# A long convolution and an MLP in one kernel: k and v loaded in rows of four tokens, and the short convolution split at the phase wrap

## The chip, the cores and the metric

The kernel runs on one core of a Trainium2 chip. The core has a tensor engine for matrix products (PE, with weight loads listed apart as PEld), a vector engine (DVE), a scalar engine (ACT), GpSimd (POOL) and a queue engine (SP), which here only issues DMA transfers. On-chip memory is SBUF (128 partitions); matrix products are written to PSUM[...]. The metric is device time in microseconds, and the figure compared is the median of several runs. One further execution is recorded by the hardware profiler, and the profile and the trace come from it.

## The reference

There are two blocks, one after the other, over 2048 tokens of 512 channels, all in bfloat16. Block A normalises the input to get q, and then computes

```
k_shift[s] = sum over t of k_pad[s + t] * shift_k[:, 3 - t]     (4 taps, causal, per channel)
kv         = k_shift * v
y          = irfft( rfft(kv padded to 4096) * rfft(ssm_k padded to 4096) )[:2048]
h          = x + q * (y + kv * ssm_D)
```

Block B is `h2 = h + relu(layernorm(h) @ w1) @ w2` with 1376 hidden columns. The part that the change touches is the first two lines: the four-tap convolution of k along the tokens, with one weight per channel and tap, and the product with v.

## The kernel before

The transforms of length 4096 are written as matrix products. Both operands of the convolution, `ssm_k` and `kv`, go through the same steps: a transpose on PE (`to_rows`, line 281), a first transform stage (`stage1`, line 310) and a second one (`stage2`, lines 328 and 330). Then the spectra are multiplied (lines 452 and 462), the inverse transform runs (lines 609, 675 and 687), the result is gated with q (lines 658 and 660), and the two layers of the MLP follow (lines 714 and 744).

The kernel is written under a manual schedule: each engine executes its instructions in the order in which the program emits them, and waits only for the data and buffers that each instruction names.

**The loads.** SP issues, in this order: the whole `ssm_k` (`sk`, 2 MB, line 96), then alternately a transposing load of 512 tokens of k and of v, four of each (lines 115, 117 and 118), and then two small loads of `ssm_D` (`draw`, line 121). The tap weights `wsh` (4 KB) are issued on ACT's queue (line 98). A transposing load puts channels on the partitions: `kT[c]` and `vT[c]` have 128 channels on the partitions, four channel groups, and the tokens of the chunk along the free axis. Each k chunk after the first is loaded with the 16 tokens ahead of it, so that the taps can reach back over the border of the chunk; in the first chunk these 16 columns are zeros (line 112).

**The tap weights.** POOL multiplies the identity by the weights and so makes `wdiag`, a diagonal 128 x 128 matrix for each of four channel groups and four taps (line 238). The products are made for two channel groups, then the table `f1` is split into a high and a low part (lines 241 to 243), and then the other two groups follow. After that POOL copies the split tables to `f2` (line 247) and negates tables for the second stage (line 250).

**The tap products.** `taps(c, h)` handles chunk c and the two channel groups 2h and 2h + 1. For each group PE adds up four products of a diagonal matrix with 512 columns of `kT[c]`, each tap reading one column further back (line 369). DVE multiplies the bank by `vT[c]` and writes the result into `kvp2`, a view of the buffer `sk`, in the order that the transform wants (line 372). The two banks are `pk0` and `pk1`; the next call of `taps` needs them free.

**The order around the change.** PE runs 22 matmuls to warm up, then transposes `sk` (32 instructions), and then goes through eight rounds. Round gb calls `taps(gb // 2, gb % 2)` and then `stage1` on a part of the `ssm_k` data. After the eighth round PE transposes the finished `kv` into `xfl`, and the second stages begin. DVE works on the tables of angles at the start (lines 198, 189, 44, 46 and 222), evacuates the first transposes (line 284), makes the second half of a table (lines 222 and 189), and only then starts the tap products of line 372. ACT makes the sine tables (line 193) and evacuates most of `stage1`.

Of the kernel before, what the change touches and what calls it, by code (L numbers as in the profile page):

```python
# [9 lines left out]
ALU = mybir.AluOpType  # L10
BF16 = mybir.dt.bfloat16
F32 = mybir.dt.float32
# [3 lines left out]
P = 128  # L16
# [40 lines left out]
def kernel(  # L57
# [13 lines left out]
    nc = tc.nc  # L71
    _, S, D = A_q.shape
    DFF = B_w1.shape[1]
    KS = A_shift_k.shape[1]
    assert S == 2048 and D == 512 and KS == 4, "kernel is specialised to S=2048, D=512, ks=4"
    NT = 16
    DC = D // P
    NFC = (DFF + P - 1) // P
    x_d, k_d, v_d, out_d = A_q[0], A_k[0], A_v[0], out[0]
# [5 lines left out]
    consts = pl.push("consts")  # L85
    slotA = pl.push("slotA")
    vp = pl.push("vp")
    early = pl.push("early")
    wp = pl.push("wp", side="right")
    kvp = pl.push("kvp", side="right")  # L90
# [2 lines left out]


    sk = early.tile([P, DC, S], BF16, name="sk")
    nc.sync.dma_start(out=sk[:], in_=A_ssm_k.rearrange("(c p) t -> p c t", p=P))
    wsh = consts.tile([P, DC, KS], BF16, name="wsh")
    nc.scalar.dma_start(out=wsh[:], in_=A_shift_k.rearrange("(r p) j -> p r j", p=P))
    dtab = consts.tile([P, 64, DC], BF16, name="dtab")
    draw = consts.tile([P, DC, 64], BF16, name="draw")  # L100
    vT = [vp.tile([P, DC, 512], BF16, name=f"vT{c}") for c in range(4)]
    CH = 512
    kT = [(kvp if c < 2 else early).tile([P, DC, CH + 16], BF16, name=f"kT{c}") for c in range(4)]
    wdiag = kvp.tile([P, DC, KS, P], BF16, name="wdiag")

    idle = vT[3][:, 0, :]
    nc.vector.memset(idle, 0.0)
    warm = psum_t.tile([P, 512], F32, tag="pk0", name="warm")
    for _ in range(22):
        nc.tensor.matmul(out=warm[:], lhsT=idle[:, 0:P], rhs=idle, start=True, stop=True)  # L110

    nc.vector.memset(kT[0][:, :, 0:16], 0.0)
    for c in range(4):
        if c == 0:
            nc.sync.dma_start_transpose(out=kT[c][:, :, 16:CH + 16], in_=k_d[0:CH, :])  # L115
        else:
            nc.sync.dma_start_transpose(out=kT[c][:], in_=k_d[CH * c - 16:CH * c + CH, :])  # L117
        nc.sync.dma_start_transpose(out=vT[c][:], in_=v_d[CH * c:CH * c + CH, :])  # L118
    for dp in range(2):
        src = bass.AP(tensor=A_ssm_D.tensor, offset=A_ssm_D.offset + 64 * dp, ap=[[0, 64], [P, DC], [1, 64]])  # L120
        nc.sync.dma_start(out=draw[64 * dp:64 * dp + 64, :, :], in_=src)
# [84 lines left out]
    t1 = early.tile([P, 64], I32, name="f1_t")  # L206
# [30 lines left out]
    for rg in range(DC):  # L237
        nc.gpsimd.tensor_tensor(out=wdiag[:, rg, :, :], in0=ident[:].unsqueeze(1).to_broadcast([P, KS, P]),
                                in1=wsh[:, rg, :].unsqueeze(2).to_broadcast([P, KS, P]), op=ALU.mult)
# [34 lines left out]
    def tap_bank(i, shape, dtype, name):  # L274
        return psum_t.tile(shape, dtype, tag=f"pk{i}", name=name)
# [55 lines left out]
                             skip_group_check=True)  # L331


    kfl = early.tile([P, 64, 2, 64], BF16, name="kfl")
    sk32 = sk[:].rearrange("p c t -> p (c t)").bitcast(F32).rearrange("p (x m) -> p x m", m=32)
    kv32 = sk[:].rearrange("p c t -> p (c t)").bitcast(F32).rearrange("p (m x) -> p m x", m=32)

# [25 lines left out]

    kvp2 = sk[:].rearrange("p c t -> p (c t)").rearrange("p (m c a e) -> p m c a e", m=32, c=DC, e=2)
    def taps(c, h):
        pss = [tap_bank(i, [P, 512], F32, "pkv") for i in range(2)]
        for i in range(2):
            for j in range(KS):
                nc.tensor.matmul(out=pss[i][:], lhsT=wdiag[:, 2 * h + i, j, :],  # L369
                                 rhs=kT[c][:, 2 * h + i, 16 - j:CH + 16 - j], start=(j == 0), stop=(j == KS - 1))  # L370
        for i in range(2):
            nc.vector.tensor_tensor(out=kvp2[:, :, 2 * h + i, 8 * c:8 * c + 8, :].rearrange("p m a e -> p a m e"),
                                    in0=pss[i][:].rearrange("p (a m e) -> p a m e", a=8, e=2),
                                    in1=vT[c][:, 2 * h + i, :].rearrange("p (a m e) -> p a m e", a=8, e=2),
                                    op=ALU.mult)

    for gb in range(8):
        taps(gb // 2, gb % 2)
        stage1(kfl, a1k_of, gb, ("AA", "AD")[gb % 2], pairs=(gb == 2))
        if gb < 6:  # L380
            cc_part()
        if gb == 1:
            negated(22, 32)
# [458 lines left out]
```

## Time and profile before

| what | value |
|---|---|
| median of 8 runs | 204.6 us (204.02 to 208.47) |
| the profiled execution's own time | 204.62 us |
| its span in the profile | 202.5 us |
| PE busy | 191.4 us (95%), 2209 matmuls |
| DVE busy | 144.9 us (72%) |
| ACT busy | 128.8 us (64%) |
| POOL busy | 85.5 us (42%) |
| tap products on PE (line 369) | 64 instructions, 15.2 us busy, mean 380 ns |
| tap products on DVE (line 372) | 16 instructions, 10.7 us busy, mean 688 ns |
| transposing loads of k and v on SP | 8 instructions, first at 1.26 us, last at 26.07 us |

The span is the time from the first to the last instruction in the trace; the profiled execution's own time contains some 2.1 us around it. Busy time is summed per engine. Matmuls overlap one another in the array, so 380 ns is the length of one from start to end and not the distance to the next. A number after a releaser ("<-") is the time for which the engine stood idle just before the instruction, and the name is what ended the wait according to the profile; when an instruction waits for several things, the profile names the last of them that it sees.

### The profile page before, as it was taken

The page shows a single profiled execution, that of the slowest core. Times are in us where ns is not written, and L with a number is a line of the kernel's source. Part 1 is how long each engine was busy: PE and PEld are TensorE (multiplying, and loading weights), DVE is VectorE, ACT ScalarE, POOL GpSimd, SP SyncE. Part 2 cuts the span into 40 slices and gives each one's busy share as a digit, 9 for nine tenths or more (in the row PEclk, how much of TensorE's full clock was granted, in tenths as well). Part 3 has the DMA queues.
Part 4 walks back from the last instruction along what each step waited for, and adds up shares of the span by engine and source line. Part 5 has one row for each costly group of instructions (what it writes and reads, how often), then busy time and mean ns, then how long its engine had stood idle before and what let it go on. Part 6 is the DMA issues. An engine that isn't in the chain of part 4 may idle for free.

```text
span 202.5 us, 5318 instructions
## 1 busy us (share of the span) xinstructions
PE 191.4 (95%) x2209; PEld 136.0 (67%) x2209; DVE 144.9 (72%) x238; ACT 128.8 (64%) x199; POOL 85.5 (42%) x121
## 2 busy tenths in 40 slices
PE   7797989999988999999999999999999999999991
PEld 2474545999987989988998877545664556544451
DVE  7988776887877998898994698959477117652131
ACT  2668898778785988885979964925570583026300
POOL 7199995000006999994959284200120002002000
PEclk9999999999999999999999999999999999999999
DMA  5999992000000007809980669753481802140011
GB/s 174 342 215 120 203 171 56 3 5 3 3 3 5 0 9 184 288 24 218 259 203 18 108 91 186 141 103 103 91 155 43 107 10 52 32 112 14 0 52 52
DMA packets 48491, 20.05 MB, mean 99 GB/s; under 512 B 43380, under 2 KB 46932, under 8 KB 48468
## 3 DMA queue, kind: packets, MB, share of 16 engines
q1 hardware_dynamic: 47940, 19.71, 47.0%
q8 instruction: 17, 0.28, 0.6%
q10 hardware_dynamic: 528, 0.00, 0.1%
q14 instruction: 6, 0.05, 0.1%
HBM read 7.08 MB, written 2.10 MB: 45 GB/s over the span
## 4 chain that ended last, share of the span: by engine, by line
PE 78%; SPq 11%; DMA 3%; ACT 2%; DVE 2%; issue 1%; ACTq 0%
PE ps1m L714 19%; PE ps2m L744 19%; PE psy L462 7%; PE psi L609 7%; PE ps2k L328 4%; SPq L115 4%; PE ps2k L330 4%; SPq L117 4%; SPq L118 4%; PE u L328 4%; PE u L330 3%; DMA kT<-in_A_k_dram 3%; PE pz L687 3%; PE ps L310 2%; PE pst L281 2%; PE pkv L369 2%
## 5 line engine op out<-in xcount | busy, mean ns | idle before, releaser
L729 ACT ACTIVATE h1T<-ps1m 128x512 bf16<-128x512 f32 (+1 forms) x44 | 25.7, 597 | 35.8 <-PE ps1m L714 35.7
L714 PE MATMUL ps1m<-xT,w 128*128 128x512 bf16 (+2 forms) x192 | 43.7, 365 | 0.4 <-DVE xT L660 0.4
L744 PE MATMUL ps2m<-w,h1T 128*128 128x512 bf16 (+3 forms) x187 | 40.8, 368 | 0.0
L687 PE MATMUL pz<-bd,ax 128*128 128x128 f32 x96 | 35.7, 410 | 0.0
L452 POOL TENSOR_TENSOR t<-usb,kf 128x320 fp32r<-128x320 f32 x32 | 28.2, 918 | 2.2 <-ACT usb L448 1.7
L452 DVE TENSOR_TENSOR t<-u,kf 128x704 fp32r<-128x704 f32 x32 | 26.7, 883 | 3.2 <-ACT usb L448 3.0
L748 DVE SCALAR_TENSOR_TENSOR o<-ps2m,rstd,xh 128x512 bf16<-128x512 f32 (+1 forms) x17 | 12.1, 718 | 22.3 <-PE ps2m L744 11.5
L744 PEld LDWEIGHTS <-h1T 128*128 128x128 bf16 (+1 forms) x187 | 16.2, 98 | 16.0
L553 POOL TENSOR_SCALAR rstd<-mv 128x4 f32<-128x4 f32 x8 | 2.5, 317 | 57.2 <-DVE mv L551 57.2
L259 ACT CAST a<-ps 128x1024 fp32r<-128x1024 f32 (+1 forms) x22 | 22.5, 1058 | 3.8 <-PE ps L310 3.8
L714 PEld LDWEIGHTS <-w 128*128 128x128 bf16 (+1 forms) x192 | 15.9, 100 | 12.1 <-DVE xT L660 0.5
L687 PEld LDWEIGHTS pz<-bd,ax 128*128 128x128 f32 x96 | 18.6, 193 | 7.6
L547 DVE BATCH_NORM_STATS2 st<-xh 128x6 f32<-128x512 bf16 x32 | 19.9, 677 | 0.5 <-DMA xh<-xT 0.5
L658 DVE TENSOR_TENSOR qT<-pz,qT 128x1024 bf16<-128x1024 f32 x8 | 9.8, 1220 | 13.7 <-PE pz L687 10.8
L259 ACT CAST kf<-psy 128x512 fp32r<-128x512 f32 x30 | 17.5, 642 | 1.8 <-PE psy L462 0.2
L537 ACT ACTIVATE bd<-ecw,nbias 32x512 fp32r<-32x512 int32 x24 | 17.3, 719 | 0.6
L369 PE MATMUL pkv<-kT,wdiag 128*128 128x512 bf16 x64 | 15.2, 380 | 1.8 <-POOL f_hi L247 1.1
L462 PE MATMUL psy<-t,ipos 128*128 128x512 f32 x48 | 16.0, 395 | 0.0
L261 DVE CAST a<-ps 128x1024 fp32r<-128x1024 f32 (+1 forms) x12 | 13.6, 1136 | 2.6 <-PE ps L310 2.5
L259 ACT CAST ax<-psi 128x1024 fp32r<-128x1024 f32 x13 | 12.4, 1014 | 3.7 <-PE psi L609 3.5
L609 PE MATMUL psi<-dre,kf 128*128 128x256 f32 x60 | 14.6, 286 | 0.0
L609 PE MATMUL psi<-dim,kf 128*128 128x256 f32 x60 | 14.3, 280 | 0.0
(132 smaller groups left out, 392.5 us busy)
## 6 DMA issues: line engine op xcount, KB each, us to landing
sk<-in_A_ssm_k_dram SPq DMA_DIRECT2D x1, 2048.0 KB
xh<-in_A_q_dram SPq DMA_DIRECT2D x16, 128.0 KB
out_dram<-o SPq DMA_DIRECT2D x15, 128.0 KB
w<-in_B_w_dram SPq DMA_DIRECT2D x1, 1376.0 KB
w<-in_B_w_dram SPq DMA_DIRECT2D x1, 1280.0 KB
xh<-xT SPq DMA_TRANSPOSE x8
out_dram<-o SPq DMA_DIRECT2D x2, 64.0 KB
w<-in_B_w_dram SPq DMA_DIRECT2D x1, 96.0 KB
```

The source lines that it names most:

```text
L259: nc.scalar.copy(out=o, in_=i)
L328: nc.tensor.matmul(out=ps[:, kk, :], lhsT=at_k1(w_re, k1), rhs=a_in(2 * k1), start=True, stop=False, skip_group_check=True)
L369: nc.tensor.matmul(out=pss[i][:], lhsT=wdiag[:, 2 * h + i, j, :], rhs=kT[c][:, 2 * h + i, 16 - j:CH + 16 - j], start=(j == 0), stop=(j == ...
L452: eng.tensor_tensor(out=t[:, :, j, :], in0=in0.unsqueeze(1).to_broadcast([P, 2, n, 2]), in1=kfr[:, :, j, ks], op=ALU.mult)
L462: nc.tensor.matmul(out=psy[:], lhsT=m_[:], rhs=t_.rearrange("p j k -> p (j k)"), start=first, stop=not first)
L537: nc.scalar.activation(out=bd[h][rows, :, :, rg, :], in_=ecw[q % 2][rows, :, 256 * h:256 * h + 256].rearrange("p b (j n) -> p b j n", n=32 ...
L547: nc.vector.bn_stats(out=st[:, i, :], in_=src[:, i, :])
L609: nc.tensor.matmul(out=banks[i // 2][:, i % 2, :], lhsT=kf[:, c, 4 * m:4 * m + 4, :].rearrange("p r k -> p (r k)"), rhs=d[:].rearrange("p ...
L687: nc.tensor.matmul(out=pz[:, il, :, a, :], lhsT=ax[:, 64 * rho + n2, :, :].rearrange("p d g -> p (d g)"), rhs=bd[h][:, rho, 4 * il + a, :, ...
L714: nc.tensor.matmul(out=ps1[fc][:fsz, 128 * ii.start:128 * ii.stop].rearrange("p (i t) -> p i t", t=P), lhsT=w1[:, c, fc * P:fc * P + fsz], ...
L729: nc.scalar.activation(out=h1T[:fsz, fc, :], in_=ps1[fc][:fsz, :], func=ACT.Relu)
L744: nc.tensor.matmul(out=ps2[:, 0:w], lhsT=h1T[:ksz, fc, i * P:(i + 1) * P], rhs=w2[:ksz, fc, ds], start=(fc == 0), stop=(fc == NFC - 1))
```

## The change

Four things are changed, and all of them are in the first 35 us.

1. `k` and `v` are read as matrices with 512 rows of 2048 elements, a row holding four consecutive tokens. A chunk is 128 such rows. The transposing load gives, for each of the four positions t in a row (the phase, the token number modulo 4) and each channel group, a block of 128 channels by 128 rows. `kT` and `vT` become one tile each, `[128, 4 phases, 4 channel groups, rows]`. All 512 rows of k stand behind one another in one tile, with 16 columns of zeros ahead, so that the overlap of 16 tokens for each chunk is no longer loaded.
2. Tap j of phase t reads phase t - j. Where t - j is negative, the token lies in the row before: phase t - j + 4, one column earlier. A tap product therefore has two parts, phases j to 3 and phases 0 to j - 1. Tap 0 has only one part with 512 columns; the others have 384 + 128, 256 + 256 and 128 + 384 columns. A call of `taps` has 14 matmuls instead of 8, each with its own weight load.
3. DVE's product with v reads the bank and `vT` by phase and writes to the same places as before.
4. The load of `wsh` is issued on SP ahead of `sk`, instead of on ACT. The tile `kfl`, which `to_rows` fills, is allocated earlier, and the warm-up matmuls read it instead of `vT[3]`.

```diff
+    kfl = early.tile([P, 64, 2, 64], BF16, name="kfl")
+    wsh = consts.tile([P, DC, KS], BF16, name="wsh")
+    nc.sync.dma_start(out=wsh[:], in_=A_shift_k.rearrange("(r p) j -> p r j", p=P))
     nc.sync.dma_start(out=sk[:], in_=A_ssm_k.rearrange("(c p) t -> p c t", p=P))
-    wsh = consts.tile([P, DC, KS], BF16, name="wsh")
-    nc.scalar.dma_start(out=wsh[:], in_=A_shift_k.rearrange("(r p) j -> p r j", p=P))
...
-    vT = [vp.tile([P, DC, 512], BF16, name=f"vT{c}") for c in range(4)]
-    CH = 512
-    kT = [(kvp if c < 2 else early).tile([P, DC, CH + 16], BF16, name=f"kT{c}") for c in range(4)]
+    CM = 128
+    vT = vp.tile([P, 4, DC, 4 * CM], BF16, name="vT")
+    kT = kvp.tile([P, 4, DC, 4 * CM + 16], BF16, name="kT")
...
-    idle = vT[3][:, 0, :]
+    idle = kfl[:, 0:4].rearrange("p g d n -> p (g d n)")
...
-    nc.vector.memset(kT[0][:, :, 0:16], 0.0)
+    nc.vector.memset(kT[:, :, :, 0:16], 0.0)
     for c in range(4):
-        if c == 0:
-            nc.sync.dma_start_transpose(out=kT[c][:, :, 16:CH + 16], in_=k_d[0:CH, :])
-        else:
-            nc.sync.dma_start_transpose(out=kT[c][:], in_=k_d[CH * c - 16:CH * c + CH, :])
-        nc.sync.dma_start_transpose(out=vT[c][:], in_=v_d[CH * c:CH * c + CH, :])
+        for dst, src, at in ((kT, k_d, 16 + CM * c), (vT, v_d, CM * c)):
+            nc.sync.dma_start_transpose(out=dst[:].rearrange("p t r m -> p (t r) m")[:, :, at:at + CM],
+                                        in_=src.rearrange("(m t) d -> m (t d)", t=4)[CM * c:CM * c + CM, :])
...
-        pss = [tap_bank(i, [P, 512], F32, "pkv") for i in range(2)]
+        pss = [tap_bank(i, [P, 4, CM], F32, "pkv") for i in range(2)]
+        at = 16 + CM * c
         for i in range(2):
+            rg = 2 * h + i
             for j in range(KS):
-                nc.tensor.matmul(out=pss[i][:], lhsT=wdiag[:, 2 * h + i, j, :],
-                                 rhs=kT[c][:, 2 * h + i, 16 - j:CH + 16 - j], start=(j == 0), stop=(j == KS - 1))
+                for t0, t1, f0, m0 in ((j, 4, 0, at), (0, j, 4 - j, at - 1)):
+                    if t0 < t1:
+                        nc.tensor.matmul(out=pss[i][:, t0:t1, :], lhsT=wdiag[:, rg, j, :],
+                                         rhs=kT[:, f0:f0 + t1 - t0, rg, m0:m0 + CM], start=(j == 0),
+                                         stop=(j == KS - 1), skip_group_check=True)
         for i in range(2):
-            nc.vector.tensor_tensor(out=kvp2[:, :, 2 * h + i, 8 * c:8 * c + 8, :].rearrange("p m a e -> p a m e"),
-                                    in0=pss[i][:].rearrange("p (a m e) -> p a m e", a=8, e=2),
-                                    in1=vT[c][:, 2 * h + i, :].rearrange("p (a m e) -> p a m e", a=8, e=2),
-                                    op=ALU.mult)
+            rg = 2 * h + i
+            nc.vector.tensor_tensor(
+                out=kvp2[:, :, rg, 8 * c:8 * c + 8, :].rearrange("p (m tp) a e -> p a m tp e", tp=2),
+                in0=pss[i][:].rearrange("p (tp e) (a m) -> p a m tp e", e=2, a=8),
+                in1=vT[:, :, rg, CM * c:CM * c + CM].rearrange("p (tp e) (a m) -> p a m tp e", e=2, a=8), op=ALU.mult)
```

## The prediction

> **What bounds the kernel now.** I first read the page's chain of work that ended last, because only its links move the end:
>
> ```profile
> PE 78%; SPq 11%; DMA 3%; ACT 2%; DVE 2%; issue 1%; ACTq 0%
> ```
>
> PE carries it nearly everywhere; the 11% of SP's queue and the 3% of DMA are the head. So I next asked for the chain in order of time, cut to 0 to 36 us (start, length, what):
>
> ```profile
> 0.72 0.48 SPq L96
> ...
> 1.26 7.53 SPq L115
> ...
> 15.67 4.75 SPq L117
> ...
> 23.68 6.18 DMA kT<-in_A_k_dram
> ...
> 29.90 1.90 PE pkv L369 x8
> 31.81 0.61 PE ps L310 x64
> 32.42 1.88 PE pkv L369 x8
> ...
> 34.33 0.70 DVE sk L372
> ...
> 35.17 0.84 PE pst L281 x6
> ```
>
> SP issues `sk` and then eight transposes, back to back; the last k chunk lands at 29.86, and from there two tap groups lead to 35.17, where the transposes of the tap products start. After 35 us the chain is PE almost throughout (ACT and DVE links of 0.5 to 1.2 us near 110 to 115), and nothing of the diff lies there. So the change in time is, to a first order, how far 35.17 moves.
>
> Is DMA alone late? The timeline of the same stretch says no:
>
> ```profile
> 13.53 1.41 DVE L222 TENSOR_SCALAR w_tc<-w_ts 128x1024 int32<-128x1024 int32 x1
> 14.97 0.69 DVE L189 TENSOR_SCALAR w_tc<-w_tc 128x1024 int32<-128x1024 int32 x1
> 15.58 1.28 DVE L372 TENSOR_TENSOR sk<-pkv,vT 128x512 bf16<-128x512 f32 x2
> 16.32 1.89 PE L369 MATMUL pkv<-kT,wdiag 128*128 128x512 bf16 x8 [1.09 <-POOL f_hi L247]
> 29.90 1.90 PE L369 MATMUL pkv<-kT,wdiag 128*128 128x512 bf16 x8 [0.63 <-DMA kT<-in_A_k_dram]
> 31.65 1.29 DVE L372 TENSOR_TENSOR sk<-pkv,vT 128x512 bf16<-128x512 f32 x2 [1.05 <-DMA vT<-in_A_v_dram]
> ```
>
> PE lost only 1.09 and 0.63 us between 12.7 and 35. The 1.09 is charged to POOL, but tap group 1 needs the bank that DVE's first product frees at 15.58 + 0.69 = 16.27: that wait is DVE's. PE and DMA therefore run within about a microsecond of each other, and help for one alone meets the other soon.
>
> The loads, from the DMA view of 15 to 24 us (40 slices of 0.225 us):
>
> ```profile
> GB/s 87 224 240 201 94 191 24 3 0 0 41 275 291 355 162 0 0 1 8 9 10 174 275 291 279 290 291 287 291 288 269 188 213 74 35 6 8 10 9 213
> q8 instruction: 2, 0.03, 1.5%
> ```
>
> The transposes run at up to 291 GB/s with holes of 0.9 to 1.4 us. Two instruction fetches fall in this view, and I read two of its three holes as theirs (a reading, not shown here); the view of 24 to 34 us has one more hole, near 28.5, and again two fetches.
>
> **What the Trainium skill says.** "DMA: Bandwidth & Descriptors", section Latency and other measured facts, gives transposes 261 GB/s with a non-contiguous middle dimension and 350 to 400 contiguous. Here the peak is 291. The later transposes of 128 rows by 16 blocks, the new shape but read from SBUF, run at 205 to 218 GB/s back to back (DMA view of 120 to 129 us). Two k/v transposes without a hole between them, issued at 8.83 and 11.03, took 2.15 and 2.61 us to issue for 0.52 MB: about the same pace. The trace does not support 350. "SBUF — State Buffer", section Who interferes with whom: DVE and GpSimd share one port pair, and the second to issue blocks for the whole instruction. The trace agrees: L222 took 1.41 us beside POOL's wdiag and 0.69 us earlier, when POOL was idle.
>
> **The change part by part.** Durations are of the profiled execution (own time 204.62, median 204.6: the sum applies to the median as it is).
>
> *wsh ahead of sk on SP.* Its issue leaves ACT's queue, where it hid, and enters SP's: 0.48 plus a gap, 0.54 us before `sk` (0.72 to 1.26). Behind `sk` stand all eight transposes; PE waits for `sk` at 9.05. wsh is 512 pieces of 8 bytes (q10 held 528 packets, 3.4% of 16 engines over 9 us: 0.3 us per engine). That data cost existed before, beside `sk`. But the two draw loads, 512 pieces of 128 bytes, trickle from 31.3 to 34.0: if pieces go out that slowly and `sk` waits, the delay D reaches 0.54 + 2.7 = 3.2. Below, D could be 0.2 if the two issues overlap. I take D = 0.8: the issue and one more quarter microsecond. The ends go into the range.
>
> *wdiag early.* POOL sat idle from 4.79 to 9.22 for wsh. With wsh landing by about 4, the first two wdiag (2.3 us) run from 4.8, the second pair after f1's split near 9.9 (f_f is done at 9.01), ending near 11.9 instead of 14.40. Then L222 at 13.5 no longer meets them: 1.41 becomes 0.69, minus 0.72 us on DVE ahead of the first products. The price: the first pair now meets DVE's table turns (L189, L198, L222, 4.4 to 9.6), 0.7 to 1.4 us by the same collision. DVE finished these at 9.63 and waited for PE's first transpose until 9.78; with `sk` later by D that cover is 0.95, so 0 to 0.45 is left. I take 0.1.
>
> *Tap matmuls.* Per group of taps, four 512-column products (216 ns apart: 8 in 1.89 us, the last 0.38 long) become one of 512, two of 384, two of 256 and two of 128, each with its own weight load; 48 more pairs in all. Spacing: 256 columns take 118 ns (L714: 25 in 3.10 us, the last 0.27); 384 between, 168. 128 columns with a weight load: "TensorE: Matmul & The Clock Gate", section Back-to-back issue gap, gives 81 ns for such pairs (its 216 ns for 512 columns agrees with the trace). Sum 216 + 2x168 + 2x118 + 2x81 = 950 against 864: +86 ns, x16 = 1.4 us, 0.17 per call of taps. Bounds: 11 ns per extra pair (118 less 256 columns at 216/512) gives 0.5; a full weight load of 98 ns each, with no overlap, gives 4.7.
>
> *Products on DVE.* The reads now step over phases in PSUM and vT. L284 already reads PSUM four elements apart by 128 words, 512 elements, in 0.69 us, as L372 does: nothing. For vT's stride I take nothing; the upper bound is doubling, 16 x 0.69, mostly under PE.
>
> *Memsets, tiles.* The kT memset grows from 32 to 128 words, about 0.1 us on DVE, inside the same 0.95 cover. vT[3]'s dependence on the warm-up matmuls goes; these end at 7.6, far ahead of its issue. The order of DMAs and later instructions is the same.
>
> *Transposes.* Same 4.2 MB, less 48 rows of overlap (0.05 MB, 0.2 us), rows of 4 KB instead of 1 KB. I take the same pace with the same holes: all land D later.
>
> *Sum.* PE path: first products at 15.58 + 0.8 + 0.1 - 0.72 = 15.76, so tap group 1 at 16.50 (+0.18). Group 6 was ready at 29.27; plus 0.18 and five groups at 0.17 gives 30.3. DMA path: 29.90 + 0.8 = 30.7, later, so it decides. Then two tap groups, +0.34: 35.17 becomes 36.3, **+1.1 us: 205.7**.
>
> **Rivals.**
> *Faster (0.20).* The long rows, or a hole that misses the last k chunk, bring that chunk before PE arrives. The hole near 28 cost about 1.4 us, and 96 more PE instructions shift the fetches. PE alone then decides. With D = 0.5 and 0.04 per call: tap group 1 at 16.2, group 6 at 29.35 (29.27 - 0.12 + 5x0.04), the end 5.27 + 0.08 later at 34.7: -0.5, 204.1. It needs kT's last chunk by about 29.3 and 128-column pairs near 64 ns. Against it: the SBUF-fed transposes with 4 KB rows are no quicker.
> *No difference (0.15).* The chunk is early, the pairs cost 0.17 per call and D is 0.3: group 1 at 16.0, group 6 at 29.8, the end at 35.4: +0.2, 204.8.
> *One more hole (0.13).* Another 1.4 us in the loads: +2.5, 207.1. For it: more instructions, hence an earlier fetch.
> *Long rows are slow to transpose (0.07).* Sixteen rows of a block now lie 4 KB apart in HBM. At 0.6 us more per chunk, 8 x 0.6 = 4.8: about 210. Nothing in this trace shows it.
>
> **How the numbers follow.** The main forecast has 0.45, its own range 205.1 to 206.7 (D from 0.2 to 1.8). Slower sums to 0.45 + 0.13 + 0.07 = 0.65, same 0.15, faster 0.20. The range 203.9 to 207.6 leaves out the slow rows and the far end of the faster case. Under 0.2% (0.4 us) is what a measurement here cannot tell from no change.
>
> **What would show it.** D: PE's first L281 at about 9.85 instead of 9.05. wdiag: POOL's first L237 near 4.8. L221's second run 0.69 us. 128-column matmuls 70 to 90 ns apart. kT's last chunk near 30.7, with PE waiting. The xfl transposes start near 36.3. I am wrong if `sk` lands as before, if the chunks come 2.0 us apart or less, or if a tap group stays at 1.9 us.

## The result and the profile after

The changed kernel takes 206.1 us (median of 12 runs, 205.65 to 208.32) where the kernel before takes 204.62 (33 runs). The medians lie 1.5 us apart; the ratio of the runs is 1.0089, with a 95% interval of 1.0067 to 1.0112, so the change makes the kernel slower. The profiled execution took 206.27 us, with a span of 204.2 (before: 202.5). The forecast was 205.7, slower.

The difference is made where the prediction looked for it: the transposes of the tap products into `xfl` start at 36.72 us instead of 35.17, 1.55 later, and the span is 1.7 longer. But the road to that point is another one. On the page of the changed kernel, these are the busy line, the chain by engine, and the two groups of `taps`:

```profile
PE 192.3 (94%) x2257; PEld 139.9 (69%) x2257; DVE 150.5 (74%) x238; ACT 129.4 (63%) x199; POOL 87.2 (43%) x121
...
PE 79%; SPq 7%; DVE 6%; DMA 3%; ACT 2%; issue 1%; ACTq 0%; DVEq 0%
...
L376 DVE TENSOR_TENSOR sk<-pkv,vT 128x512 bf16<-128x512 f32 x16 | 16.4, 1066 | 1.3 <-DMA vT<-in_A_v_dram 0.6
L371 PE MATMUL pkv<-kT,wdiag 128*128 128x128 bf16 (+3 forms) x112 | 15.7, 288 | 1.4 <-DVE sk L376 1.4
```

The same two groups in the kernel before:

```profile
L372 DVE TENSOR_TENSOR sk<-pkv,vT 128x512 bf16<-128x512 f32 x16 | 10.7, 688 | 5.0 <-PE pkv L369 3.5 <-DMA vT<-in_A_v_dram 1.5
L369 PE MATMUL pkv<-kT,wdiag 128*128 128x512 bf16 x64 | 15.2, 380 | 1.8 <-POOL f_hi L247 1.1
```

One number stands out: DVE's product with v takes 1066 ns instead of 688, on the same 512 elements, 16 times: 16.4 us instead of 10.7. DVE's total busy time grew by 5.6 us (144.9 to 150.5), which is this line. The 48 extra matmuls, on the other hand, added 0.5 us of busy PE (15.2 to 15.7). The DVE share of the chain went from 2% to 6%. PE does not stand idle longer before its taps than it did (1.4 us against 1.8), but all of this wait is now for a bank that DVE has not emptied.

The chain of the changed kernel in order of time (start, length, what), from the loads to the `xfl` transposes:

```profile
14.62 6.80 DMA vT<-in_A_v_dram
...
21.51 1.06 DVE sk L376
...
22.61 1.05 PE pkv L371 x7
...
23.69 2.09 DVE sk L376 x2
25.78 0.86 DVE a L260
...
26.82 1.08 DVE sk L376
...
27.95 2.02 PE pkv L371 x14
...
31.04 1.86 PE pkv L371 x14
...
33.51 1.00 PE pkv L371 x7
...
34.53 2.06 DVE sk L376 x2
...
36.72 3.88 PE pst L280 x32
```

In the kernel before, the last chunk of k ended this stretch and PE went straight through two groups of taps. Now a chunk of v comes first: it lands at 21.42, DVE takes it up at 21.51, and from there DVE and PE hand the lead to each other. (DVE waited for this chunk in the kernel before too. The trace keeps the times at which transfers land: there it was 20.64, and DVE's product started at 20.73 after 0.57 us of idle time. The profile charges that wait to PE, whose bank had been complete since 19.80.) PE waits for a bank that DVE has not yet emptied, and DVE is late because each product is 0.38 us longer. At the end, both products of the last round stand after PE (2.06 us), where before one stood there (0.70). The `kT` link at 23.68 is gone from the chain.

The timeline of DVE in the changed kernel (start, length, form, count, idle time before and what ended it):

```profile
5.46 1.01 DVE L44 TENSOR_SCALAR f_t<-f_r,n1c 128x32 int32<-128x32 int32 x1
6.50 0.96 DVE L46 TENSOR_SCALAR f_t<-f_t 128x32 int32<-128x32 int32 x1
...
11.23 3.08 DVE L283 TENSOR_SCALAR kfl<-pst 128x512 int32<-128x512 int32 x5
14.22 0.68 DVE L221 TENSOR_SCALAR w_tc<-w_ts 128x1024 int32<-128x1024 int32 x1
...
15.55 4.22 DVE L376 TENSOR_TENSOR sk<-pkv,vT 128x512 bf16<-128x512 f32 x4
...
21.51 4.27 DVE L376 TENSOR_TENSOR sk<-pkv,vT 128x512 bf16<-128x512 f32 x4 [0.61 <-DMA vT<-in_A_v_dram]
...
26.82 4.25 DVE L376 TENSOR_TENSOR sk<-pkv,vT 128x512 bf16<-128x512 f32 x4
```

DVE starts its first product at 15.55, as before (15.58). From then to 36.6 the timeline notes idle time on it only twice: 0.61 us for v's second chunk, and 0.25 us for the last taps. In this stretch DVE is a bound, although it is busy for only 74% of the whole span.

PE in the changed kernel:

```profile
9.49 4.08 PE L280 MATMUL pst<-ident,sk 128*128 128x128 f32 x32 [1.83 <-POOL f_hi L240]
13.41 1.91 PE L371 MATMUL pkv<-kT,wdiag 128*128 128x512 bf16 x14
...
16.61 2.04 PE L371 MATMUL pkv<-kT,wdiag 128*128 128x512 bf16 x14 [0.67 <-DVE sk L376]
...
22.61 2.02 PE L371 MATMUL pkv<-kT,wdiag 128*128 128x512 bf16 x14 [0.49 <-DVE sk L376]
```

And in the kernel before:

```profile
9.05 3.83 PE L281 MATMUL pst<-ident,sk 128*128 128x128 f32 x32 [1.50 <-DMA sk<-in_A_ssm_k_dram]
```

The first transposes of `sk` start at 9.49 instead of 9.05. (The profile charges the wait to POOL; these transposes read `sk` and the identity, which POOL had finished at 4.5, and `sk` landed at 9.36, against 8.92 before. So the wait is for `sk`.) A call of `taps` of 14 matmuls takes 1.91 us, against 1.89 for 8 before.

Where the time is lost can be read from the starts of the eight calls of `taps`. They are later than in the kernel before by 0.69, 0.29, 0.44, 1.02, 1.02, 1.18, 1.07 and 1.05 us, and the `xfl` transposes by 1.55. Most of the first 0.69 vanishes in the wait for the first bank. The delay then grows in two steps: at the fourth call, after v's second chunk, and at the end, where two slow products stand after PE.

### The profile page after: what moved, and what is told of

It is laid out like the page before. It is cut to its first block, busy times and chain, and to the rows that moved or that the text cites. A ratio compares the mean times of both kernels' runs of the same rounds, so it can differ in the third digit from the quotient of the medians.

```text
span 204.2 us, 5412 instructions
## 1 busy us (share of the span) xinstructions
PE 192.3 (94%) x2257; PEld 139.9 (69%) x2257; DVE 150.5 (74%) x238; ACT 129.4 (63%) x199; POOL 87.2 (43%) x121
## 4 chain that ended last, share of the span: by engine, by line
PE 79%; SPq 7%; DVE 6%; DMA 3%; ACT 2%; issue 1%; ACTq 0%; DVEq 0%
PE ps1m L718 19%; PE ps2m L748 19%; PE psy L466 7%; PE psi L613 7%; SPq L116 6%; PE ps2k L327 4%; PE ps2k L329 4%; PE u L327 4%; DMA vT<-in_A_v_dram 3%; PE u L329 3%; DVE sk L376 3%; PE pkv L371 3%; PE ps L309 3%; PE pz L691 3%; PE pst L280 2%; ACT bd L541 1%
## 5 line engine op out<-in xcount | busy, mean ns | idle before, releaser
L752 DVE SCALAR_TENSOR_TENSOR o<-ps2m,rstd,xh 128x512 bf16<-128x512 f32 (+1 forms) x17 | 11.9, 716 | 20.3 <-PE ps2m L748 8.9
L718 PEld LDWEIGHTS <-w 128*128 128x128 bf16 (+1 forms) x192 | 15.9, 100 | 12.1 <-DVE xT L664 0.5
L691 PEld LDWEIGHTS pz<-bd,ax 128*128 128x128 f32 x96 | 18.6, 193 | 7.6
L376 DVE TENSOR_TENSOR sk<-pkv,vT 128x512 bf16<-128x512 f32 x16 | 16.4, 1066 | 1.3 <-DMA vT<-in_A_v_dram 0.6
L371 PE MATMUL pkv<-kT,wdiag 128*128 128x128 bf16 (+3 forms) x112 | 15.7, 288 | 1.4 <-DVE sk L376 1.4
L260 DVE CAST a<-ps 128x1024 fp32r<-128x1024 f32 (+1 forms) x12 | 13.6, 1136 | 2.6 <-PE ps L309 2.6
```

Of the source, the lines that this page charges most:

```text
L371: nc.tensor.matmul(out=pss[i][:, t0:t1, :], lhsT=wdiag[:, rg, j, :], rhs=kT[:, f0:f0 + t1 - t0, rg, m0:m0 + CM], start=(j == 0), stop=(j = ...
L376: nc.vector.tensor_tensor(out=kvp2[:, :, rg, 8 * c:8 * c + 8, :].rearrange("p (m tp) a e -> p a m tp e", tp=2), in0=pss[i][:].rearrange("p ...
L691: nc.tensor.matmul(out=pz[:, il, :, a, :], lhsT=ax[:, 64 * rho + n2, :, :].rearrange("p d g -> p (d g)"), rhs=bd[h][:, rho, 4 * il + a, :, ...
L718: nc.tensor.matmul(out=ps1[fc][:fsz, 128 * ii.start:128 * ii.stop].rearrange("p (i t) -> p i t", t=P), lhsT=w1[:, c, fc * P:fc * P + fsz], ...
```

## The experiments

After the traces there were four candidates for the 1.5 us: (V) `vT` is read with a step of 4 KB between neighbouring elements, (P) the PSUM bank is read with a step, (W) `wsh` stands ahead of `sk` on SP, and (S) the taps are split. What the prediction had put first was W and S.

### The two steps of DVE's product, apart

All four kernels are the changed one with other access patterns. In the kernels called `_flat`, and further down in `x_loads_only` and `x_before_step`, the products no longer belong to the tokens in whose places they are written; the amount of work is the same.

Both operands read in runs (`x_both_flat`):

```diff
...
-in0=pss[i][:].rearrange("p (tp e) (a m) -> p a m tp e", e=2, a=8),
-in1=vT[:, :, rg, CM * c:CM * c + CM].rearrange("p (tp e) (a m) -> p a m tp e", e=2, a=8), op=ALU.mult)
+in0=pss[i][:].rearrange("p t (h m tp e) -> p t h m tp e", h=2, tp=2, e=2),
+in1=vT[:, :, rg, CM * c:CM * c + CM].rearrange("p t (h m tp e) -> p t h m tp e", h=2, tp=2, e=2), op=ALU.mult)
```

The view of the output, left out here, is rewritten to match; the same places are written in the same order.

> The changed kernel, but DVE's product (L376) reads the PSUM bank and vT in the order in which they lie, in runs of 128 elements, and writes to the same places in the same order; tokens are paired wrongly, the work is the same in size. Stride theory (the stepping reads made DVE the bound and carry most of the 1.5 us): L376 back from 1.07 to about 0.69 us, PE's wait for the banks gone, the xfl transposes start near 35.6 instead of 36.7 (bound by v's last chunk at about 32.1), time about 205.0. Late-load theory (sk later and the split taps carry it, DVE hidden behind them): L376 shorter, but the time stays at about 206.0.

Measured: 219.29 us, ratio 1.0689 [1.0649, 1.0729]. The end time was a miss, and it can't be used. With `vT` as one tile and this view of it, the first product waits for the last chunk of v, though it reads only the first (called the false wait below). The chain of this kernel shows it:

```profile
25.03 4.44 DMA vT<-in_A_v_dram
...
29.55 0.70 DVE sk L376
```

The first product starts at 29.55 instead of 15.55, and PE, whose two banks stay full, stands still for 14.4 us. What can be used is the length of the product: 691 ns (mean of 16).

Only `vT` read in runs, the bank still with its step (`x_v_flat`, the second line of the diff above):

> As the run with both reads in order, but only vT is read in order; the PSUM bank is still read with a step of 128 words (tokens paired wrongly, same work). If vT's step (4 KB from element to element) is the cost: L376 about 0.69 us, time about 205.0. If the PSUM step is the cost: L376 stays at 1.07, time 206.1. If both count: about 0.85 to 0.9.

Measured: 220.11 us, ratio 1.0745 [1.0717, 1.0773], with the same unusable end. The group of products:

```profile
L376 DVE TENSOR_TENSOR sk<-pkv,vT 128x512 bf16<-128x512 f32 x16 | 10.9, 690 | 20.5 <-DMA vT<-in_A_v_dram 14.1
```

Only the bank read in runs, `vT` still with its step (`x_psum_flat`, the first line of the diff):

> The other half: the PSUM bank is read in order, vT still with steps of 4 KB (tokens paired wrongly, same work). If vT's step is the cost: L376 stays at 1.07 us and the time at 206.1. If the PSUM step is: 0.69 and about 205.0. L283 read PSUM with the same step at 0.69 us with one operand, so I expect vT.

Measured: 205.49 us, ratio 1.0054 [1.0035, 1.0072]. The group of products:

```profile
L376 DVE TENSOR_TENSOR sk<-pkv,vT 128x512 bf16<-128x512 f32 x16 | 16.4, 1067 | 1.0 <-DMA vT<-in_A_v_dram 0.4
```

The table of two by two is complete: 1066 ns with both steps, 690 without `vT`'s, 1067 without the bank's, 691 without either. The whole 0.38 us is `vT`'s step; P falls as a cause of the longer product. This kernel is still 0.6 us quicker than the changed one by the medians, 0.4 if each is compared with the kernel before in its own series. In its profile v's second chunk lands 0.2 earlier, at 21.21, and the `xfl` transposes start at 36.33 instead of 36.72. The other 0.2 goes with a pause of PE: in the changed kernel it stands still for 0.28 us at 30.47, in the middle of `stage1`, which the profile puts down to no engine, and here it doesn't. Why the chunk is earlier and the pause gone is open.

The step moved from DVE's read to PE's write (`x_psum_order`): the bank is laid out with the phase innermost, PE writes with a step of 4 words, DVE reads the bank in runs (its view, left out here, follows the new layout) and `vT` still with its step.

```diff
-pss = [tap_bank(i, [P, 4, CM], F32, "pkv") for i in range(2)]
+pss = [tap_bank(i, [P, CM, 4], F32, "pkv") for i in range(2)]
-nc.tensor.matmul(out=pss[i][:, t0:t1, :], lhsT=wdiag[:, rg, j, :],
+nc.tensor.matmul(out=pss[i][:, :, t0:t1].rearrange("p m t -> p t m"), lhsT=wdiag[:, rg, j, :],
...
```

> The changed kernel with the tap matmuls writing their bank with the phase innermost (a step of four words on PE's side), so that DVE reads PSUM in order and vT stepping; result unchanged. If the PSUM step is DVE's cost, 0.69 us and about 205.0; if vT's, L376 stays at 1.07 and the time at 206.1. If a stepping write slows PE, a call of taps grows from 1.85 us and the time goes above 206.1.

Measured: 217.36 us, ratio 1.0611 [1.0590, 1.0631]. DVE's products stay at 1048 ns, and PE pays for the step. Its group, on the page of this kernel:

```profile
L371 PE MATMUL pkv<-kT,wdiag 128*128 128x128 bf16 (+3 forms) x112 | 29.0, 449 | 0.0
```

A call of `taps` takes 3.56 us in the chain instead of 1.86, and the eight calls come to 13.6 us more, about the whole loss (13.0). Here the wait goes the other way: DVE stands still 12.1 us for PE.

### The parts of the change, alone

`wsh` ahead of `sk` in the kernel before (`x_before_wsh`):

```diff
+wsh = consts.tile([P, DC, KS], BF16, name="wsh")
+nc.sync.dma_start(out=wsh[:], in_=A_shift_k.rearrange("(r p) j -> p r j", p=P))
 nc.sync.dma_start(out=sk[:], in_=A_ssm_k.rearrange("(c p) t -> p c t", p=P))
-wsh = consts.tile([P, DC, KS], BF16, name="wsh")
-nc.scalar.dma_start(out=wsh[:], in_=A_shift_k.rearrange("(r p) j -> p r j", p=P))
```

> The kernel before with one part of the change: wsh issued on SP ahead of sk. Theory (sk 0.44 us later, all transposes behind it the same, wdiag early): first L281 at 9.5 instead of 9.05, the last k chunk near 30.3, the xfl transposes at 35.6, time about 205.0 (+0.4). Rival (the early wdiag takes the collision off DVE and that decides): first products 0.7 us earlier against PE, 204.2 or less.

Measured: 204.74 us, ratio 1.0002 [0.9978, 1.0026], less than the 205.0 expected. The chain of this kernel:

```profile
15.88 3.89 SPq L117
...
21.91 7.82 DMA kT<-in_A_k_dram
...
29.78 1.90 PE pkv L369 x8
...
35.06 3.88 PE pst L281 x32
```

PE's first transposes are 0.31 later (9.36), but the transposing load that took 4.75 us to issue before takes 3.89 here, and the last chunk of k lands at 29.74, not later than before. With the old access patterns the delay of the loads comes to nothing that can be measured; the interval reaches 0.5 us either way.

The same edit taken back in the changed kernel (`x_wsh_act`, the diff above reversed):

> The changed kernel with wsh back on ACT's queue, behind sk: wdiag starts near 9.2 again, L221 collides again (1.4 us). Stride theory: DVE's products still decide; they start at about 15.6 as now, and v's second chunk lands 0.4 earlier, so the end moves by 0 to -0.4: 205.7 to 206.1. Late-load theory: -0.8, 205.3.

Measured: 205.50 us, ratio 1.0044 [1.0029, 1.0059], between what the two theories gave. Its chain:

```profile
23.18 2.06 DVE sk L376 x2
...
33.80 2.10 DVE sk L376 x2
...
36.04 3.88 PE pst L280 x32
```

No DMA is left between 16 and 36 us, the wait for v's second chunk is gone, and DVE leads from product to product. Against the changed kernel this is 0.6 us less (206.1 - 205.5; in the profiles 36.72 - 36.04 = 0.68), close to the 0.61 that DVE waited for v. The other 0.9 us remain with `wsh` in its old place.

It does not follow that the wait is `wsh`'s delay passed on. These are the issues of v's second chunk and of the load behind it, first in the changed kernel, then here:

```profile
14.62 1.76 SPq L116 DMA_TRANSPOSE vT<-in_A_v_dram  x1
16.42 4.76 SPq L116 DMA_TRANSPOSE kT<-in_A_k_dram  x1
...
14.71 3.01 SPq L116 DMA_TRANSPOSE vT<-in_A_v_dram  x1
17.76 2.19 SPq L116 DMA_TRANSPOSE kT<-in_A_k_dram  x1
```

The changed kernel issued the chunk 0.09 us earlier, and it landed 1.37 us later (21.42 against 20.05). A pause of the transfers, one of the prediction's holes, fell before its end, from about 18.6 to 19.9; here none comes between the issue and 22.3. With `wsh` ahead in the kernel before, the chunk landed at 20.11, earlier than the 20.64 without. So W is worth about 0.6 us in this pair of kernels, and whether the place of `wsh` moves the pause, or something else does, is open.

The split of the taps in the kernel before (`x_before_split`), in parts of the same sizes:

```diff
-nc.tensor.matmul(out=pss[i][:], lhsT=wdiag[:, 2 * h + i, j, :],
-                 rhs=kT[c][:, 2 * h + i, 16 - j:CH + 16 - j], start=(j == 0), stop=(j == KS - 1))
+for a0, a1 in ((0, CH - 128 * j), (CH - 128 * j, CH)):
+    if a0 < a1:
+        nc.tensor.matmul(out=pss[i][:, a0:a1], lhsT=wdiag[:, 2 * h + i, j, :],
+                         rhs=kT[c][:, 2 * h + i, 16 - j + a0:16 - j + a1], start=(j == 0),
+                         stop=(j == KS - 1), skip_group_check=True)
```

> The kernel before with its tap matmuls cut as in the change (512; 384 + 128; 256 + 256; 128 + 384 columns, 14 per call), everything else as before. What the changed kernel's trace says (1.85 us per call against 1.83): +0.05 to +0.1 in all, 204.7. What was forecast (0.17 per call, two calls on the path): 204.95.

Measured: 204.83 us, ratio 1.0001 [0.9981, 1.0022]. In its chain a call takes 1.87 us, and the end moves by 0.12:

```profile
32.55 1.88 PE pkv L371 x14
...
35.29 3.88 PE pst L281 x32
```

S is free to within the measurement, whose interval reaches from -0.4 to +0.5 us.

The loads of four-token rows alone (`x_loads_only`): the changed kernel with `wsh` back on ACT, unsplit taps, and both operands of the product read in runs as in `x_both_flat`. Of its edit, the taps:

```diff
-for t0, t1, f0, m0 in ((j, 4, 0, at), (0, j, 4 - j, at - 1)):
...
+nc.tensor.matmul(out=pss[i][:], lhsT=wdiag[:, rg, j, :], rhs=kT[:, :, rg, at - j:at - j + CM],
+                 start=(j == 0), stop=(j == KS - 1))
```

> Only the loads of the change: k and v in rows of four tokens into one tile each, but uncut taps of 512 columns, products that read in order, and wsh on ACT (tokens paired wrongly, the same amount of work). If the row length does nothing to the transposes: 204.6, as before. If rows of 4 KB are quicker: chunks closer than 2.4 us and 204.2 or less. If slower: above 205.

Measured: 220.07 us, ratio 1.0728 [1.0688, 1.0769], with the false wait for v's last chunk again. Only the loads can be read. From its SP timeline (start and length of each issue), the shortest issues:

```profile
8.79 2.32 SPq L116 DMA_TRANSPOSE vT<-in_A_v_dram  x1
...
17.67 2.20 SPq L116 DMA_TRANSPOSE kT<-in_A_k_dram  x1
19.92 2.17 SPq L116 DMA_TRANSPOSE vT<-in_A_v_dram  x1
...
24.77 2.07 SPq L116 DMA_TRANSPOSE vT<-in_A_v_dram  x1
```

They take 2.07 to 2.32 us, and the four shortest in the kernel before 1.95 to 2.61, so the long rows show themselves neither quicker nor slower to transpose. The three others took 2.59 to 3.33 us here, and 3.18 to 4.75 before. With PE standing still the gaps are fewer, and the last transpose is issued by 26.8 instead of 29.5. That fits the reading that fetches of instructions make the holes; it doesn't show it.

### The step alone, and the step removed

The kernel before, with only `vT[c]` read with a step of 128 elements, 256 bytes (`x_before_step`).

```diff
...
-in0=pss[i][:].rearrange("p (a m e) -> p a m e", a=8, e=2),
-in1=vT[c][:, 2 * h + i, :].rearrange("p (a m e) -> p a m e", a=8, e=2),
+in0=pss[i][:].rearrange("p (a m tp e) -> p a m tp e", a=8, tp=2, e=2),
+in1=vT[c][:, 2 * h + i, :].rearrange("p (tp e a m) -> p a m tp e", tp=2, e=2, a=8),
```

> The kernel before with one thing added: the product reads v with a step of 128 elements (256 bytes) instead of in order (tokens paired wrongly, same work; loads, taps and wsh as before). Stride theory: L372 grows from 0.69 to about 1.07 us, DVE becomes the bound, and the time goes to 205.5 to 205.9 by that alone. If a step of 256 bytes costs less than one of 4 KB, less. Late-load theory: the products hide under PE, 204.6.

Measured: 205.79 us, ratio 1.0052 [1.0037, 1.0067]. The page's groups for this kernel:

```profile
L369 PE MATMUL pkv<-kT,wdiag 128*128 128x512 bf16 x64 | 15.5, 380 | 1.9 <-DVE sk L372 1.9
L372 DVE TENSOR_TENSOR sk<-pkv,vT 128x512 bf16<-128x512 f32 x16 | 16.3, 1061 | 0.7 <-PE pkv L369 0.3
```

And its chain:

```profile
33.72 2.03 DVE sk L372 x2
...
35.89 3.88 PE pst L281 x32
```

This is the decisive run. One access pattern, with loads, `wsh` and taps untouched, gives 1061 ns, the lead of DVE, PE's wait for DVE alone (1.9 us, where the 1.8 of the kernel before had two causes), and 1.0 us of the 1.5 (205.79 - 204.76, the kernel before beside it; the interval is 0.8 to 1.4). A step of 256 bytes costs what a step of 4 KB costs.

The changed kernel with v in four tiles, read in runs (`x_v_tiles_flat`), so that neither the step nor the false wait is there. The product reads `vT[c]` in runs as in `x_v_flat`.

```diff
-vT = vp.tile([P, 4, DC, 4 * CM], BF16, name="vT")
+vT = [vp.tile([P, 4, DC, CM], BF16, name=f"vT{c}") for c in range(4)]
-for dst, src, at in ((kT, k_d, 16 + CM * c), (vT, v_d, CM * c)):
+for dst, src, at in ((kT, k_d, 16 + CM * c), (vT[c], v_d, 0)):
...
```

> The changed kernel with v in four tiles, one per chunk, and the product reading v in order (tokens paired wrongly, same work); the tiles keep each product waiting for its own chunk only, which the earlier runs with v in order did not. PSUM is still read stepping. Stride theory: L376 at 0.69 us, no wait for the banks on PE, the end bound by the loads again: 204.7 to 205.1. Late-load theory: 205.7 or more.

Measured: 205.43 us, ratio 1.0036 [1.0016, 1.0055]. The products are back at 689 ns, and in the chain PE leads from 18.2 to 35.5. Removing the step thus gives 0.7 us of the 1.5; I had expected more, and the time lies between the two theories again. In the profiled execution (205.95 us) the rest can be seen: PE, which had stood still for 1.9 us before `sk` came, ran at half its clock just then. Windows of 1 us (the window, its length, then busy time and instructions of PE, PEld, DVE, ACT and POOL, and last PE's granted clock, the DMA share and GB/s):

```profile
10.00:11.00 1.00, 1.00 (x11) 1.00 (x10) 0.96 (x2) 0.48 (x2) 0.94 (x3) 0.89 0.78 177
11.00:12.00 1.00, 1.00 (x6) 1.00 (x5) 1.00 (x3) 0.59 (x2) 1.00 (x1) 0.50 0.97 183
```

The 32 transposes took 5.44 us instead of 4.08 in the changed kernel, the first product came at 17.47, and the `xfl` transposes at 36.39. But the runs of this kernel with a mean clock of 0.995 or more took 205.3 us in the median too, so the dip is not the whole of its 0.7 us above the kernel before. That remainder is open.

Last, a try to keep the loads and lose the step in the product (`x_by_e`): each product is cut in two by the parity of the phase. The reads run along the tokens, and single elements are written 1 KB apart, where the other kernels write pairs 512 bytes apart.

```diff
...
+for e in range(2):
+    nc.vector.tensor_tensor(
+        out=kvp2[:, :, rg, 8 * c:8 * c + 8, e].rearrange("p (m tp) a -> p tp a m", tp=2),
+        in0=pss[i][:].rearrange("p (tp e) (a m) -> p e tp a m", e=2, a=8)[:, e],
+        in1=vT[:, :, rg, CM * c:CM * c + CM].rearrange("p (tp e) (a m) -> p e tp a m", e=2, a=8)[:, e],
+        op=ALU.mult)
```

> The changed kernel with each product cut in two, by parity of the token: both halves read PSUM and vT in runs of 128, and write single elements 1 KB apart; result unchanged. If only stepping reads cost: two of about 0.43 us (256 elements and the fixed part), 0.86 against 1.07, and about 205.2. If stepping writes cost as much: two of 0.6 us or more, and above 207.

Measured: 226.24 us, ratio 1.1035 [1.0982, 1.1088]. The group, 256 elements each:

```profile
L377 DVE TENSOR_TENSOR sk<-pkv,vT 128x256 bf16<-128x256 f32 x32 | 37.1, 1477 | 0.0
```

The step has only moved to the write, where it costs more: 5.8 ns for an element instead of 2.1 (each the whole instruction divided by its elements). The same with `wsh` on ACT (`x_by_e_act`):

> The same cut products, and wsh back on ACT's queue, which alone took 0.5 us off the changed kernel: 204.7 if the reads alone cost, above 206.5 if the writes do. Under 204.4 it would beat both kernels.

Measured: 226.45 us, ratio 1.1073 [1.1039, 1.1107]. With DVE so far behind, the place of `wsh` doesn't matter. None of the kernels is faster than the kernel before.

## Why the prediction was right, and where it was wrong

The sign and the size held (205.7 forecast, 206.1 measured), but they came out of two terms that were too large and one that had been set to nothing. That what was missing in one was about made up by the others is luck.

**"Products on DVE" is the step that failed.** It set `vT`'s stride to nothing and gave doubling, "mostly under PE", as the upper bound. The measured product is 1066 ns for 688: 0.38 x 16 = 6.0 us on DVE (5.7 of busy time, as neighbours overlap). The cover was thinner than the step assumed. A pair of rounds asks 4 x 1.07 = 4.3 us of DVE for products and about 1.1 for the cast at L260, so 5.4; the trace has 26.82 to the next such start at 32.26, 5.44. PE needs 2 x (1.86 + 0.61) = 4.9, or 5.3 when `stage1`'s larger part (1.00 us) falls in the pair. The price thus turned DVE from an engine with a slack of 1 us or more a pair into the bound. What this did can be read at the end: the last taps start at 33.51 instead of 32.42 (+1.09), and from there to the `xfl` transposes it is 3.21 us instead of 2.75 (+0.46), because two products stand after PE's first bank. The evidence the step used, L284, was of a stepped read of PSUM, and for PSUM it was right (`x_psum_flat`: 1067 against 1066). It was carried over to SBUF without a row of the trace that showed that.

The Trainium skill has the missing price in kind: "Advanced Engine Details and Errata", section Memory Cachelines, says that SBUF has 16-byte lines, that at least two hits on a line are needed to absorb the access latency, and that a different line on each access is penalised. The runs agree: every element of `vT` lies in another line, with 256 bytes as with 4 KB, and both cost 0.38 us for 512 elements. The page gives no size. Of PSUM, the same section says that any pattern that isn't contiguous slows matmuls significantly; `x_psum_order` agrees (1.86 to 3.56 us), while DVE's reads of PSUM with a step are free here.

**"wsh ahead of sk on SP": right in kind, its size and its way to the end off.** D measured 0.44 (0.26 to 0.54 in other kernels with the same edit), not 0.8. The way was to be the last chunk of k, with PE waiting; it landed at 30.45 (29.86 before), but it is not in the chain, and PE came for it only at 30.97. Instead v's second chunk landed 0.78 later than before, and a DVE that had become the bound waited 0.61 for it. `x_wsh_act` puts the edit at 0.6 us, `x_before_wsh` at nothing, within 0.5 us, where DVE has slack. That the 0.6 us is D passed on is not shown: the pause of the transfers fell at another place.

**"wdiag early": right in sum.** POOL's first `wdiag` came at 4.76 (forecast 4.8), the second pair ended at 13.2 (11.9), and L221's second run took 0.68 us. The price was larger than its upper end: L44 and L46 took 1.01 and 0.96 us beside POOL instead of 0.22 and 0.18, and DVE reached its first `kfl` copy at 11.23 instead of 9.78. The five copies then ran back to back, so that L221 began only 0.69 us later than before (14.22 against 13.53), and its 0.68 us instead of 1.41 made that good: the first product came at 15.55 (forecast 15.76). The lock between DVE and POOL that the prediction cited shows here on instructions of a fifth of a microsecond: with `wsh` alone moved (`x_before_wsh`) L44 and L46 take the same 1.01 and 0.96, and with it moved back (`x_wsh_act`) 0.22 and 0.18.

**"Tap matmuls": the direction right, the size wrong by a factor of eight.** Forecast 0.17 us per call, measured 0.02: 1.85 us from the start of a call to the start of `stage1`, against 1.83. The 81 ns that the Trainium skill gives for a pair of 128 columns ("TensorE: Matmul & The Clock Gate", section Back-to-back issue gap) is too much here. In that section 81 ns stands for a sustained stream and the 216 ns for a single matmul; the forecast took one of each kind. The extra in a group of taps is 10 ns instead of 86, so a group takes 874 ns. That is 3 ns for each of the three extra pairs, below the 11 of the lower bound too (10 by the bound's own figures, 118 less 108). If each part takes time in proportion to its columns (162 ns for 384, 108 for 256, from 216 for 512), a 128-column part has (874 - 216 - 2 x 162 - 2 x 108) / 2 = 59 ns; with the forecast's 168 and 118, only 43. Either way most of an extra weight load (98 ns) is hidden. The named sign of error, "a tap group stays at 1.9 us", is what happened.

**"Transposes": right.** All eight issues are within 0.40 us of their length before, with the same long ones among them (4.76 and 4.75), and all start 0.3 to 0.9 later. The 291 GB/s called the peak is not the highest value in the line that the prediction shows: one slice has 355. Fetches of instructions fall in the same view, so whether the transposes alone reached it is open. **"Memsets, tiles": right**, nothing of it shows.

**"Sum": wrong in its parts.** DMA was to decide with 30.7 and the split to add 0.34. In place of +0.8, +0.3 and 0, the runs give about 0.6 for W (beside V only, with its way open), 0 for S within the interval, and 0.9 to 1.0 for V. V and W do not seem to add: without V no cost of W was found. V itself is 1.0 alone in the kernel before, 0.9 in the changed one with `wsh` on ACT, and 0.7 is what its removal gives with `wsh` on SP.

The rivals: "Faster" asked for 128-column pairs near 64 ns, and 43 to 59 came. It also asked for the last k chunk by 29.3, and that landed at 30.45. It fell with the products as well, since PE came for the chunk only at 30.97; and `x_v_tiles_flat`, where these take their old time, was still 0.36% slower than the kernel before, so no run shows that side. "No difference" is outside the measured interval. "One more hole" and "slow long rows" did not occur.

## What to carry to other kernels

A load in another layout moves the cost to those who read the tile: for each reader and writer, look at the step between neighbouring elements, and price it from a row with the same memory and the same step, or as open. An engine beside the path covers an increase only up to its slack in that very stage, counted per round, and that slack was about 1 us in 5 here although the engine was idle a quarter of the whole span. A late load that costs nothing while its consumer has slack is paid for once the consumer has none; how late it is can depend on where the pauses of the transfers fall, so compare the landing of the very chunk and not only the order of the issues.

## What the runs showed of the hardware that was not expected

- DVE's product of PSUM and bf16 SBUF data takes 1.35 ns for an element when SBUF is read in runs, 2.08 when every element lies 256 bytes or 4 KB from the last, the same for both steps. Both figures are whole instructions divided by their elements. A step of 128 words in the read of PSUM adds nothing (1066 against 1067, 690 against 691). In all of these, pairs of bf16 are written 512 bytes apart; single bf16 elements written 1 KB apart come to 5.8 ns each (1477 ns for 256).
- PE writing PSUM with a step of four words runs at about half its rate: 3.56 us instead of 1.86 for a call of 14 matmuls.
- PE's clock fell to 0.50 for 3.4 us, from about 10.8 to 14.2, in the one profiled run of `x_v_tiles_flat`, after PE had stood still for 1.9 us (7.4 to 9.3); in the changed kernel, idle for 1.83 us at the same place, it stayed at 1.00. "TensorE: Matmul & The Clock Gate" of the Trainium skill, section What's actually happening, names an idle window of about 3.4 us for this; the wait here was shorter.
